# Pack attention and two feed-forward layers: batch 0's pack products to the split tiles, rows by head and pack

## The chip, the cores and the metric

The kernel runs on one core of one Trainium2 chip. The metric is device microseconds of one execution, from the first to the last instruction with what lies around it; times are compared between runs of the same chip.

## The reference

The program computes attention through 32 packed queries per head, then a dense feed-forward layer with squared ReLU, then a top-1 mixture of eight experts:

```python
# q, k, v: (8 batches, 8 heads, 576, 64); p: (8, 8, 32, 64); x: 4608 tokens of 512
p_packed = sm_attn(p, k, v)              # softmax(p k^T / 8) v : 32 rows per head
out = sm_attn(q, p_packed, p_packed)     # softmax(q p_packed^T / 8) p_packed
...
h = np.maximum(x @ w_in, 0.0)            # w_in 512 x 2048, w_out 2048 x 512, float64 inputs
x = (h * h @ w_out).astype(np.float32)
...
logits = x @ w_gate + modality_bias[modality_id]
e_idx = np.argmax(logits, axis=1)
...
    h = np.maximum(x[mask] @ w1[e], 0.0)
    out[mask] = gate_w[mask, None] * (h @ w2[e])
```

## The kernel before

**Stages.** (1) The packing loop, `i` = 0 to 18, takes 16 quads (half a batch, four heads): scores, softmax, turning on TensorE, values; the result is `pp32` and, compacted, `ppq`. (2) Unit 0 and then units 1 to 11: each is 384 tokens, 16 steps `f` of 128 hidden columns. (3) The mixture of experts.

**The pack products.** The second attention and `w_in` are joined: out @ w_in is the softmax weights (256 per token: 8 heads x 32 packs) times `p_packed @ w_in` per head. So `pw_quad(bq, u, eng)` multiplies four batches' packed rows (128 partitions: 4 batches x 32 packs) of two heads (pair `hp`) by 512 hidden columns (`fb`), copies the result out of PSUM into a tile `pws` (three buffers) and writes it to DRAM, `pw_d`. There are 32 such products, in the order of the list `due`. `load_pw(b, fb)` reads one batch's 256 rows by 512 columns back into a tile `praw` (two buffers, shared with `abuf`), and `split_pw(b, f)` makes of 128 columns of it the high and low half with which `layer1` multiplies (`head`, `ring`). Row order: pack and then head.

**Second attention.** `att2(u)` is a generator: scores `s`, softmax in the tile `e`, turning (`ta`), copies to `a2T`. Unit 0's weights are made in the packing loop, unit 1's during unit 0.

**Weights.** `w_in` and `w_out` come as float64 words. `load_in`/`load_out` fetch a block, `conv_in`/`conv_out` convert it (one ScalarE scaling, three VectorE passes), `halve_out` splits a `w_out` block for `layer2`. Before, blocks 0 to 12 of `w_in` are converted in the packing loop, one per iteration, 13 to 15 in steps 0 to 2 of unit 0.

**Order.** The packing loop and unit 0 stand under a manual schedule: each engine runs its instructions in the order of the code. SyncE issues the loads in that order too. From unit 1 on a scheduler orders them. In step `f` of unit 0: part of `att2(1)`, `layer1(0, f)`, one or two products, `layer2` of the step before, the halves of `w_out` block `f`, conversions, `split_pw(0, f + 2)`.

Of the kernel before, what the change touches and what calls it, by code (L numbers as in the profile page):

```python
# [26 lines left out]
def tile_pack_attention_moe_moe2(  # L27
# [25 lines left out]
    NDC = DM // P  # L53
    NPC = H * NPK // P
    MAIN = 4 * P
    LAST = S - MAIN
# [82 lines left out]
    kbuf = [t.rearrange("p (g s) -> p g s", g=2) for t in kbuf]  # L139
    pn = a_p.tile([P, B, HP, NPK], F32, name="pn", bufs=1)  # L140
    ptb = [a_p.tile([P, HP, 2 * NPK], F32, tag="ptb", name="ptb", bufs=2) for _ in range(2)]
# [9 lines left out]

    pw_d = tc.dram_tile([DFF // 512, B, NPK, H, 512], F32, name="pw_d")
    x2_d = tc.dram_tile([NT, XR], F32, name="x2_d")
# [54 lines left out]

    RAWS_IN = [stage[:, i % 4] for i in range(13)]
    RAWS_IN += [rows[:, KW : KW + 1024], wgf[:, 2048:3072], wgf[:, 3072:]]  # L210
    RAWS_OUT = [wgf[:, :1024], wgf[:, 1024:2048], rows[:, :1024]]

# [26 lines left out]
    def load_out(u):  # L239
        if u < NU:  # L240
            nc.sync.dma_start(words(RAWS_OUT[u % 3]), w_out32[u * P : (u + 1) * P])

    def conv_in(u):
        return convert(wi[4 + u // HP][:, u % HP], words(RAWS_IN[u]))

# [14 lines left out]

    praw = {}
    def load_k(i):
# [101 lines left out]
    def pw_quad(bq, u, eng):  # L364
# [16 lines left out]
        so = pw_p.tile([P, 2, 512], F32, tag="w5", name="pws", bufs=3)  # L381
        dst = pw_d[fb, 4 * bq : 4 * bq + 4].rearrange("b n h f -> (b n) h f")[:, 2 * hp : 2 * hp + 2]
        if both is None:
# [4 lines left out]
        else:  # L388
            nc.vector.tensor_copy(so, both)
        (nc.scalar if eng == "ACT" else nc.sync).dma_start(dst, so)  # L390

# [11 lines left out]
    def load_pw(b, fb):  # L403
        raw = w_p.tile([P, NPC, 512], F32, tag="raw", name="praw")
        nc.sync.dma_start(raw, pw_d[fb, b].rearrange("(c n) h f -> (n h) c f", c=NPC))
        praw[b, fb] = raw

# [22 lines left out]

    def att2(u, fine=False):
        hl = held["at"].tile([P, 2, NPC, UW], F32R, tag="a2T", name="a2T", bufs=2)
        a2T[u] = hl
        for r in range(UT):
# [17 lines left out]
            nc.vector.tensor_reduce(out=mx, in_=s2v, axis=AX.X, op=ALU.max)  # L452
            et = held["at"].tile([P, NPK, H], F32, tag="e", name="e", bufs=1)
            e = et.rearrange("p n h -> p h n")
            nc.vector.tensor_tensor(
# [14 lines left out]
            ta = bank("t", "ta2")  # L470
            ef = et.rearrange("p n h -> p (n h)")
            for c in range(NPC):
                nc.tensor.transpose(ta[:, c * P : (c + 1) * P], ef[:, c * P : (c + 1) * P], ident)
            if fine:
                yield "turned"
            tv = ta[:, : NPC * P].rearrange("p (c n) -> p c n", c=NPC)
# [428 lines left out]
    with tc.manual_schedule():  # L905
# [6 lines left out]
        turn_p(1)  # L912
        bg = att2(0, True)
        setup = setup_routing(x2_p)
        todo = [(conv_in, u) for u in range(13)] + [(conv_out, 0), (conv_out, 1)]
        cv = iter(())
        due = [*range(13), 16, 17, 13, 14, 15, *range(18, 32)]

# [10 lines left out]
        for i in range(NQ + 3):  # L929
# [9 lines left out]
            if i < NQ:  # L939
                scores(i)  # L940
                if i < 2:
                    qts[i * P] = load_q(i * P)
                load_k(i + 3)
                load_v(i)
                if i < 13:
                    load_in(i)
                elif i < 15:
                    load_out(i - 13)
                greatest(i)
            if i >= 3 and todo:  # L950
                cv = start_conv()
# [8 lines left out]
            if i == 16:  # L960
                load_in(13)
            if i in (9, 11, 15):
# [5 lines left out]
            if i == 17:  # L968
                load_pw(0, 0)
                load_in(14)  # L970
            if i == 18:
                halve_out(0)
                load_out(2)
                load_in(15)
# [22 lines left out]
        for f in range(NF):  # L997
            turned = None
            if f:
                load_out(f + 3)  # L1000
                turned = next(bg, None)
            hl = layer1(0, f)
            if turned:
                next(bg)
            if f == 0:
                split_pw(0, 1)
            pw_next("tt")
            if f < 9:
                pw_next("th")
            if pend is not None:  # L1010
                if f == 1:
                    held["acc"] = [bank("acc", "acc") for _ in range(UT)]
                layer2(held["acc"], *pend)
            pend = (f, hl)
            if f:
                halve_out(f)
            if f == 0:
                compact(NQ - 1)
            if 0 < f < NU - 1:
                for _ in conv_out(f + 1):  # L1020
                    pass
            if f < 3:
                for _ in conv_in(13 + f):
                    pass
            if f + 2 < NF:
                split_pw(0, f + 2)
            if f in (0, 3, 6):
                load_pw(0, 1 + f // 3)
            ahead(0, 0, f)
# [129 lines left out]
```

## Time and profile before

| | |
|---|---|
| median of 3 runs | 1249.94 us (1247.66 to 1254.98) |
| profiled execution | 1249.71 us, of which the span 1247.9 |
| TensorE busy | 1198.6 us, 96% |
| VectorE, ScalarE, GpSimd busy | 818.4, 637.8, 289.0 us |
| DMA, first 80 us | mean 355 GB/s |

PE is TensorE, PEld its weight loads, DVE VectorE, ACT ScalarE, POOL GpSimd, SP SyncE; a name with a q (ACTq, SPq) is that engine's queue of DMA and semaphore instructions. In a row of the timeline, the bracket holds how long the engine stood idle before and what the profile names as releaser. The granted clock (PEclk) is a share of full speed, 2.4 GHz; 0.50 is the lower level, 1.2 GHz.

### The profile page before, as it was taken

To read this page: it belongs to the slowest core of one execution; us is meant where nothing else is said; L and a number is where in the kernel's file an instruction comes from. 1 tells how busy PE (TensorE), PEld (TensorE's weight loads), DVE (VectorE), ACT (ScalarE), POOL (GpSimd) and SP (SyncE) were. 2 spreads that over 40 slices of the span, in tenths; PEclk is the share of its full clock that TensorE was granted. 3 is DMA by queue.
4 is the path that set the end of the run, shared out by engine and by line. 5 is a ranking of instruction groups with operands and counts; after the bars stand their busy time and mean duration, and the time that the engine had idled before them with its cause. 6 is when DMAs were issued, how large, how long until landed. Compare 5 with 4: busy or idle time off the path is not lost.

```text
span 1247.9 us, 17648 instructions
## 1 busy us (share of the span) xinstructions
PE 1198.6 (96%) x6036; PEld 980.4 (79%) x6036; DVE 818.4 (66%) x2122; ACT 637.8 (51%) x1332; POOL 289.0 (23%) x347
## 2 busy tenths in 40 slices
PE   7998999999999999999999999999999999999995
PEld 5764568888888888878888888877888888888884
DVE  5766778776859867695876697788454354354331
ACT  5576567765567665477654666523243243233220
POOL 2204465231123330032310223003022023023001
PEclk9999899999999999999999999999999999999998
DMA  9998774211112210112201013324263253264211
GB/s 338 362 336 314 273 239 147 77 35 63 51 34 69 66 72 17 35 60 86 76 28 44 26 44 121 111 102 154 76 204 130 74 203 136 68 204 141 71 61 36
DMA packets 71221, 149.21 MB, mean 120 GB/s; under 512 B 5712, under 2 KB 25296, under 8 KB 70992
## 3 DMA queue, kind: packets, MB, share of 16 engines
q1 hardware_dynamic: 64208, 124.61, 29.1%
q0 software_dynamic: 5760, 19.17, 4.7%
q10 hardware_dynamic: 1152, 4.19, 0.8%
q8 instruction: 49, 0.80, 0.3%
q14 instruction: 52, 0.43, 0.1%
HBM read 112.01 MB, written 35.95 MB: 119 GB/s over the span
## 4 chain that ended last, share of the span: by engine, by line
PE 72%; DVE 14%; DMA 7%; issue 3%; ACT 3%; POOL 1%; POOLq 0%; SPq 0%; DVEq 0%; ACTq 0%
PE acc L520 23%; PE h L810 16%; PE o L832 15%; PE ph L494 10%; DVE rows L541 5%; DMA early<-in_v 2%; PE s L441 2%; DMA rows<-in_k 2%; DVE r L507 1%; DMA wraw<-in_moe_w 1%; PE tr L790 1%; PE pw L374 1%; DVE ghl L513 1%; PE ph L502 1%; PE ph L503 1%
## 5 line engine op out<-in xcount | busy, mean ns | idle before, releaser
L520 PE MATMUL acc<-wb,ghl 128*128 128x512 f32 x1728 | 445.4, 401 | 3.6 <-ACT ghl L511 2.5
L520 PEld LDWEIGHTS acc<-wb,ghl 128*128 128x128 f32 x1728 | 320.9, 190 | 76.4 <-ACT ghl L511 7.6
L541 DVE SCALAR_TENSOR_TENSOR rows<-rows,wgb 128x512 f32<-128x512 f32 x288 | 213.2, 740 | 3.5
L810 PE MATMUL h<-xt,wb 128*128 128x512 f32 x864 | 213.6, 397 | 1.0 <-DVE ht L821 1.0
L810 PEld LDWEIGHTS h<-xt,wb 128*128 128x128 f32 x864 | 161.9, 188 | 40.3 <-DVE ht L821 1.9
L513 DVE TENSOR_TENSOR ghl<-r,ghl 128x384 fp32r<-128x384 f32 x176 | 107.3, 610 | 72.5 <-ACT ghl L511 72.3
L511 ACT ACTIVATE ghl<-r 128x384 fp32r<-128x384 f32 x192 | 100.0, 522 | 74.7 <-PE acc L520 72.1
L821 DVE SCALAR_TENSOR_TENSOR ht<-h,ht 128x512 fp32r<-128x512 f32 x72 | 49.4, 689 | 119.2 <-ACT ht L820 119.1
L820 ACT ACTIVATE ht<-h 128x512 fp32r<-128x512 f32 x72 | 42.4, 592 | 148.5 <-PE h L810 148.3
L832 PE MATMUL o<-head,ht 128*128 128x512 f32 x432 | 113.4, 397 | 3.0 <-ACT ht L820 2.6
L843 POOL DMA_INDIRECT out<-wgb,idx_s x36 | 36.5, 1015 | 343.4 <-DVE wgb L841 255.6
L832 PE MATMUL o<-ring,ht 128*128 128x512 f32 x432 | 112.5, 395 | 0.0
L509 ACT ACTIVATE r<-ph 128x384 f32<-128x384 f32 x128 | 62.1, 486 | 79.5 <-PE ph L494 53.4
L510 ACT ACTIVATE r<-r 128x384 f32<-128x384 f32 x192 | 100.2, 524 | 4.6
L832 PEld LDWEIGHTS o<-head,ht 128*128 128x128 f32 x432 | 80.1, 188 | 22.5 <-ACT ht L820 3.9
L412 POOL TENSOR_TENSOR ring<-praw,ring 128x256 fp32r<-128x256 f32 x70 | 61.6, 881 | 152.8 <-ACT ring L411 152.7
L832 PEld LDWEIGHTS o<-ring,ht 128*128 128x128 f32 x432 | 80.2, 188 | 16.7
L494 PE MATMUL ph<-a2T,ring 128*128 128x384 f32 x420 | 85.8, 341 | 0.0
L494 PEld LDWEIGHTS ph<-a2T,ring 128*128 128x128 f32 x420 | 74.4, 188 | 4.3
L412 POOL TENSOR_TENSOR head<-praw,head 128x256 fp32r<-128x256 f32 x58 | 52.1, 899 | 102.3 <-ACT head L411 102.1
L494 PE MATMUL ph<-a2T,head 128*128 128x384 f32 x348 | 73.5, 346 | 0.4 <-POOL head L412 0.2
L747 DVE TENSOR_TENSOR wb<-wraw,wb 128x1024 fp32r<-128x1024 f32 x36 | 44.1, 1224 | 40.6 <-ACT wb L746 40.1
(204 smaller groups left out, 1680.0 us busy)
## 6 DMA issues: line engine op xcount, KB each, us to landing
wraw<-in_moe_w SPq DMA_DIRECT2D x72, 512.0 KB, 3.7
praw<-pw_d SPq DMA_DIRECT2D x32, 512.0 KB, 3.6
pw_d<-pws SPq DMA_DIRECT2D x24, 512.0 KB, 3.8
x_d<-rows SPq DMA_DIRECT2D x12, 792.0 KB, 3.5
qT<-in_q SPq DMA_DIRECT2D x36, 256.0 KB, 2.9
early<-in_v SPq DMA_DIRECT2D x16, 512.0 KB, 9.5
stage<-in_moe_w_in SPq DMA_DIRECT2D x13, 512.0 KB, 9.4
rows<-in_k SPq DMA_DIRECT2D x10, 576.0 KB, 9.0
```

The lines of the kernel that those rows point to most:

```text
L412: nc.gpsimd.tensor_tensor(out=t[:, 1], in0=raw, in1=t[:, 0].bitcast(F32), op=ALU.subtract)
L494: nc.tensor.matmul(ph, t[:, x, c, :], a[:, y, c, :], start=(i == 0), stop=(i == 3 * NPC - 1))
L509: nc.scalar.activation(out=r, in_=ph if len(ps) == 1 else r, func=AF.Relu)
L510: nc.scalar.activation(out=r, in_=r, func=AF.Square)
L511: nc.scalar.activation(out=hl[:, 0], in_=r, func=AF.Copy)
L513: eng.tensor_tensor(out=hl[:, 1], in0=r, in1=hl[:, 0].bitcast(F32), op=ALU.subtract)
L520: nc.tensor.matmul(acc[t], hl[:, x, t * P : (t + 1) * P], w_out_block(f)[:, y, :], start=(f == 0 and x == 0 and y == 0), stop=(f == NF - 1 ...
L541: nc.vector.scalar_tensor_tensor(out=junk, in0=row[:, t, :DM], scalar=1.0, in1=wgb[:, e], op0=ALU.mult, op1=ALU.mult, accum_out=one)
L747: nc.vector.tensor_tensor(out=t[:, 1, :], in0=raw, in1=t[:, 0, :].bitcast(F32), op=ALU.subtract)
L810: nc.tensor.matmul(ph, half1(g, c)[:, x, f * P : (f + 1) * P], xs[c][:, y, :], start=(i == 0), stop=(i == 3 * NDC - 1),)
L821: nc.vector.scalar_tensor_tensor(out=h[:, 1, :], in0=ph, scalar=0.0, in1=h[:, 0, :].bitcast(F32), op0=ALU.max, op1=ALU.subtract)
L832: nc.tensor.matmul(po, hs[f][:, x, t * P : (t + 1) * P], second(f)[:, y, :], start=(i == 0), stop=(i == 3 * NFE - 1),)
```

## The change

It does five things.

- Every product is put out by SyncE, in the next iteration of the loop or in the same step of unit 0 (`put`); before, those of iterations 11 to 17 and one more were written from ScalarE's queue.
- Of the 16 products that hold batches 0 to 3, the 32 partitions of batch 0 go straight to batch 0's `praw` tiles, one DMA for each head; the other 96 go to `pw_d`. The first two of these tiles lie in `wgf` and in `pn`, and batch 0 is not loaded from DRAM.
- Rows stand by head and pack, in `e`, in `pw_d` and in `praw`. A later batch is loaded by four DMAs of 32 partitions.
- `w_in` block 13 is converted in the loop; 14 and 15 in steps 0 and 2. The `w_out` blocks 0 and 1 come an iteration later, and some buffers change place.
- Steps 0 and 1 of unit 0 have one product, steps 2 to 10 two (before: 0 to 8 two). The generator for unit 1 no longer pauses between turning and copies.

```diff
-    pn = a_p.tile([P, B, HP, NPK], F32, name="pn", bufs=1)
+    pn = pw_p.tile([P, B, HP, NPK], F32, name="pn")
...
-    pw_d = tc.dram_tile([DFF // 512, B, NPK, H, 512], F32, name="pw_d")
+    pw_d = tc.dram_tile([DFF // 512, H, B, NPK, 512], F32, name="pw_d")
...
-    RAWS_IN = [stage[:, i % 4] for i in range(13)]
-    RAWS_IN += [rows[:, KW : KW + 1024], wgf[:, 2048:3072], wgf[:, 3072:]]
-    RAWS_OUT = [wgf[:, :1024], wgf[:, 1024:2048], rows[:, :1024]]
+    RAWS_IN = [stage[:, i % 4] for i in range(14)] + [rows[:, KW : KW + 1024], wgf[:, 2048:3072]]
+    RAWS_OUT = [wgf[:, :1024], rows[:, :1024], wgf[:, 3072:]]
...
-    praw = {}
+    praw = {
+        (0, 0): wgf[:, 1024:2048].rearrange("p (c f) -> p c f", c=NPC),
+        (0, 1): pn.rearrange("p b g n -> p (b g n)").rearrange("p (c f) -> p c f", c=NPC),
+    }
+    puts = []
...
-        (nc.scalar if eng == "ACT" else nc.sync).dma_start(dst, so)
+        puts.append((bq, fb, hp, so))
+
+    def put():
+        while puts:
+            bq, fb, hp, so = puts.pop(0)
+            own = NPK if bq == 0 else 0
+            for j in range(2 if own else 0):
+                c, k = divmod(2 * hp + j, HC)
+                nc.sync.dma_start(praw[0, fb][k * NPK : (k + 1) * NPK, c], so[:own, j])
+            dst = pw_d[fb, 2 * hp : 2 * hp + 2, 4 * bq : 4 * bq + 4].rearrange("h b n f -> (b n) h f")
+            nc.sync.dma_start(dst[own:], so[own:])
...
-        raw = w_p.tile([P, NPC, 512], F32, tag="raw", name="praw")
-        nc.sync.dma_start(raw, pw_d[fb, b].rearrange("(c n) h f -> (n h) c f", c=NPC))
-        praw[b, fb] = raw
+        raw = praw[b, fb] = w_p.tile([P, NPC, 512], F32, tag="raw", name="praw")
+        for k in range(HC):
+            nc.sync.dma_start(raw[k * NPK : (k + 1) * NPK], pw_d[fb, k::HC, b].rearrange("c n f -> n c f"))
...
-            et = held["at"].tile([P, NPK, H], F32, tag="e", name="e", bufs=1)
-            e = et.rearrange("p n h -> p h n")
+            e = held["at"].tile([P, H, NPK], F32, tag="e", name="e", bufs=1)
...
-        todo = [(conv_in, u) for u in range(13)] + [(conv_out, 0), (conv_out, 1)]
+        todo = [(conv_in, u) for u in range(14)] + [(conv_out, 0), (conv_out, 1)]
...
-        due = [*range(13), 16, 17, 13, 14, 15, *range(18, 32)]
+        due = [*range(15), 16, 17, 15, *range(18, 32)]
...
+            put()
...
-                load_pw(0, 0)
-                load_in(14)
+                load_out(2)
...
-            if f < 9:
+            if 1 < f < 11:
                 pw_next("th")
+            put()
...
-            if f < 3:
-                for _ in conv_in(13 + f):
+            if f in (0, 2):
+                for _ in conv_in(14 + f // 2):
                     pass
...
-            if f in (0, 3, 6):
-                load_pw(0, 1 + f // 3)
```

Where the instructions stand. First ScalarE in iteration 12 of the packing loop and the start of 13, before (`pws<-pw` copies a product out, `atbuf<-ta` copies the turned block; the names in brackets are the counters that an instruction waits for, DMAHW0 to 7 those of the DMAs):

```order
L337 ACTIVATE atbuf<-ta 128x512 [waits PE_49]
L362 ACTIVATE ppq<-pp_85 64x2x32 [waits DVE_49] x2
L312 ACTIVATE abuf,sm<-s_700,mx 128x576 [waits DVE_49]
L215 ACTIVATE stage<-stage 128x512 [waits DMAHW7_49]
L325 ACTIVATE abuf<-abuf,sm 128x576 [waits DVE_49,Activation_49]
L387 ACTIVATE pws<-pw 128x1024 [waits PE_49]
L390 DMA pw_d<-pws 128x1024 [waits DMAHW2_49,Activation_49]
L337 ACTIVATE atbuf<-ta 128x512 [waits PE_49]
```

and in the changed kernel:

```order
L341 ACTIVATE atbuf<-ta 128x512 [waits PE_49]
L366 ACTIVATE ppq<-pp_85 64x2x32 [waits DVE_49] x2
L316 ACTIVATE abuf,sm<-s_699,mx 128x576 [waits DVE_49]
L215 ACTIVATE stage<-stage 128x512 [waits DMAHW7_49]
L329 ACTIVATE abuf<-abuf,sm 128x576 [waits DVE_49,Activation_49]
L392 ACTIVATE pws<-pw 128x1024 [waits PE_49]
L341 ACTIVATE atbuf<-ta 128x512 [waits PE_49]
```

The DMA is gone from between the copies. Second SyncE in iterations 12 and 13, in the changed kernel (`early<-in_v` are values, `stage` a `w_in` block, `wgb<-pws` the pieces of batch 0):

```order
L269 DMA wgb<-in_k 128x2x576 [waits DMAHW2_49,PE_49]
L278 DMA early<-in_v 128x1024 [waits DMAHW3_49]
L281 DMA early<-in_v 64x256 [waits DMAHW4_49]
L237 DMA stage<-in_moe_w_in 128x1024 [waits DMAHW5_49,DVE_49,Activation_49]
L403 DMA wgb<-pws 32x512 [waits DMAHW6_49,Activation_49]
L403 DMA wgb<-pws 32x512 [waits DMAHW7_49]
L405 DMA pw_d<-pws 96x2x512 [waits DMAHW0_49]
L278 DMA early<-in_v 128x1024 [waits DMAHW1_49,PE_49]
L281 DMA early<-in_v 64x256 [waits DMAHW2_49,PE_49]
L237 DMA stage<-in_moe_w_in 128x1024 [waits DMAHW3_49,DVE_49,Activation_49]
```

The three DMAs of a product now stand behind the loads of the next iteration and ahead of those after it, and take three of the eight counters. Third VectorE from the end of the packing loop to step 1 of unit 0, before (`pws<-pw` with 512 columns is VectorE's half of a product of unit 0, `wi` a `w_in` block, `tf` a `w_out` block in conversion):

```order
L389 COPY pws<-pw 128x1024
L385 COPY pws<-pw 128x512 x2
L217 TENSOR_SCALAR wi_114<-rows 128x512
L218 SCALAR_TENSOR_TENSOR wi_114<-rows,wi_114 128x512
L222 SCALAR_TENSOR_TENSOR wi_114<-rows,wi_114 128x512
L452 TENSOR_REDUCE mx<-s_1091 128x8
L455 TENSOR_TENSOR e<-s_1091,mx 128x8x32
L385 COPY pws<-pw 128x512 x2
L217 TENSOR_SCALAR tf<-rows 128x512
L218 SCALAR_TENSOR_TENSOR tf<-rows,tf 128x512
L222 SCALAR_TENSOR_TENSOR tf<-rows,tf 128x512
L217 TENSOR_SCALAR wi_114<-wgb 128x512
```

and in the changed kernel:

```order
L394 COPY pws<-pw 128x1024
L217 TENSOR_SCALAR tf<-rows 128x512
L218 SCALAR_TENSOR_TENSOR tf<-rows,tf 128x512
L222 SCALAR_TENSOR_TENSOR tf<-rows,tf 128x512
L390 COPY pws<-pw 128x512
L217 TENSOR_SCALAR wi_114<-rows 128x512
L218 SCALAR_TENSOR_TENSOR wi_114<-rows,wi_114 128x512
L222 SCALAR_TENSOR_TENSOR wi_114<-rows,wi_114 128x512
L467 TENSOR_REDUCE mx<-s_1104 128x8
L469 TENSOR_TENSOR e<-s_1104,mx 128x256
L390 COPY pws<-pw 128x512
L217 TENSOR_SCALAR tf<-wgb 128x512
```

One `w_out` conversion has come ahead of the first product half, each step has one half instead of two, and behind step 1's `w_out` conversion no `w_in` conversion follows.

## Rows read from the trace of the kernel before

**Rows 1.** Busy time (us, instructions) of each engine by stretch, granted clock, DMA share, GB/s.

```profile
core 0: us, PE busy (x) PEld busy (x) DVE busy (x) ACT busy (x) POOL busy (x), PEclk, DMA share, GB/s
63.10:72.20 9.10, 7.21 (x39) 4.71 (x37) 3.34 (x9) 4.75 (x11) 0.73 (x3) 0.81 1.04 379
78.80:84.10 5.30, 5.30 (x39) 3.62 (x37) 4.01 (x11) 3.78 (x9) 0.00 (x0) 1.00 1.05 362
107.00:112.00 5.00, 5.00 (x18) 3.62 (x15) 1.70 (x2) 2.77 (x6) 1.46 (x2) 0.66 1.05 397
126.00:134.00 8.00, 7.32 (x18) 3.52 (x17) 3.57 (x7) 3.93 (x8) 1.33 (x2) 0.50 0.91 326
200.00:235.00 35.00, 33.59 (x187) 28.76 (x185) 34.90 (x101) 23.56 (x59) 12.47 (x12) 1.00 0.24 76
```

**Rows 2.** Timeline of TensorE: start and duration in us, operation, idle time before it.

```profile
65.99 1.90 PE L300 MATMUL s<-rows,ptb 128*64 128x288 f32 x8 [0.94 <-ACT abuf L312]
```

**Rows 3.** Timeline of ScalarE and its queue, iterations 12 to 15 of the loop.

```profile
58.93 1.01 ACT L387 ACTIVATE pws<-pw 128x1024 f32<-128x1024 f32 x1
63.67 0.35 ACTq L390 DMA_DIRECT2D pw_d<-pws  x1
64.07 0.60 ACT L337 ACTIVATE atbuf<-ta 128x512 f32<-128x512 f32 x1 [4.13 <-PE ta L331]
...
71.41 0.60 ACT L337 ACTIVATE atbuf<-ta 128x512 f32<-128x512 f32 x1 [3.30 <-PE pq L347]
...
76.12 0.33 ACTq L390 DMA_DIRECT2D pw_d<-pws  x1
...
79.81 1.00 ACT L387 ACTIVATE pws<-pw 128x1024 f32<-128x1024 f32 x1
```

**Rows 4.** Timeline of SyncE's queue: one w_in load.

```profile
69.17 0.34 SPq L237 DMA_DIRECT2D stage<-in_moe_w_in  x1
```

**Rows 5.** The DMA issues of that moment: count, KB each, us to landing.

```profile
stage<-in_moe_w_in SPq DMA_DIRECT2D x1, 512.0 KB, 6.9
```

**Rows 6.** Timeline of TensorE, steps 1 to 5 of unit 0.

```profile
101.29 1.68 PE L494 MATMUL ph<-a2T,head 128*128 128x384 f32 x6
...
106.44 1.28 PE L374 MATMUL pw<-wi,ppq 64*128 64x512 f32 x4 [2.42 <-DVE e L455]
...
111.24 1.23 PE L494 MATMUL ph<-a2T,head 128*128 128x384 f32 x6
...
116.50 1.22 PE L494 MATMUL ph<-a2T,head 128*128 128x384 f32 x6
...
125.10 0.66 PE L473 MATMUL ta<-ident,e 128*128 128x128 f32 x2 [3.17 <-DVE e L466]
...
135.67 0.56 PE L441 MATMUL s<-pp,qT 128*64 128x64 f32 x6
```

**Rows 7.** Timeline of VectorE, steps 1 to 3 of unit 0.

```profile
113.79 0.42 DVE L217 TENSOR_SCALAR wi<-wgb 128x512 int32<-128x512 int32 x1
...
116.29 1.27 DVE L385 COPY pws<-pw 128x512 f32<-128x512 f32 x2
...
124.34 0.62 DVE L466 TENSOR_TENSOR e<-e,sm 128x256 f32<-128x256 f32 x1
```

**Rows 8.** Timeline of TensorE, steps 10 and 11 of unit 0.

```profile
164.97 1.23 PE L494 MATMUL ph<-a2T,ring 128*128 128x384 f32 x6
...
169.39 1.23 PE L494 MATMUL ph<-a2T,ring 128*128 128x384 f32 x6
```

**Rows 9.** Groups by line and shape: count, busy us, mean ns, idle us before.

```profile
L455 DVE TENSOR_TENSOR e<-s,mx 128x256 f32<-128x256 f32 x36 | 23.7, 658 | 0.7
...
L479 DVE TENSOR_TENSOR a2T<-ta,a2T 128x256 fp32r<-128x256 f32 x36 | 14.9, 418 | 11.2 <-ACT a2T L478 9.3 <-PE pw L374 1.8
```

**Rows 10.** DMA issues of the whole span: loads of product tiles.

```profile
praw<-pw_d SPq DMA_DIRECT2D x32, 512.0 KB, 3.6
```

**Rows 11.** Busy time of the second layer's matmuls (line 520), columns as in rows 1.

```profile
250.00:300.00 50.00, 35.00 (x140) 25.58 (x138) 1.00 0.17 59
```

More of the change, by code (lines that the diff above doesn't have):

```diff
@@ L54, in tile_pack_attention_moe_moe2 @@
     NPC = H * NPK // P
+    HC = P // NPK
     MAIN = 4 * P
@@ L381, in pw_quad @@
         so = pw_p.tile([P, 2, 512], F32, tag="w5", name="pws", bufs=3)
-        dst = pw_d[fb, 4 * bq : 4 * bq + 4].rearrange("b n h f -> (b n) h f")[:, 2 * hp : 2 * hp + 2]
+        if bq == 0 and (0, fb) not in praw:
+            praw[0, fb] = w_p.tile([P, NPC, 512], F32, tag="raw", name="praw")
         if both is None:
@@ L429, in load_q, with att2 @@
         return qT
-    def att2(u, fine=False):
+    def att2(u, fine=False, apart=False):
         hl = held["at"].tile([P, 2, NPC, UW], F32R, tag="a2T", name="a2T", bufs=2)
@@ L470, in att2 @@
             ta = bank("t", "ta2")
-            ef = et.rearrange("p n h -> p (n h)")
+            ef = e.rearrange("p h n -> p (h n)")
             for c in range(NPC):
                 nc.tensor.transpose(ta[:, c * P : (c + 1) * P], ef[:, c * P : (c + 1) * P], ident)
-            if fine:
-                yield "turned"
+            if apart:
+                yield
             tv = ta[:, : NPC * P].rearrange("p (c n) -> p c n", c=NPC)
@@ L912, in tile_pack_attention_moe_moe2 @@
         turn_p(1)
-        bg = att2(0, True)
+        bg = att2(0, True, True)
         setup = setup_routing(x2_p)
-        todo = [(conv_in, u) for u in range(13)] + [(conv_out, 0), (conv_out, 1)]
+        todo = [(conv_in, u) for u in range(14)] + [(conv_out, 0), (conv_out, 1)]
         cv = iter(())
-        due = [*range(13), 16, 17, 13, 14, 15, *range(18, 32)]
+        due = [*range(15), 16, 17, 15, *range(18, 32)]
         def start_conv():
@@ L944, in tile_pack_attention_moe_moe2 @@
                 load_v(i)
-                if i < 13:
+                if i < 14:
                     load_in(i)
-                elif i < 15:
-                    load_out(i - 13)
+                else:
+                    load_out(i - 14)
                 greatest(i)
+            put()
             if i >= 3 and todo:
@@ L960, in tile_pack_attention_moe_moe2 @@
             if i == 16:
-                load_in(13)
+                load_in(14)
             if i in (9, 11, 15):
@@ L997, in tile_pack_attention_moe_moe2 @@
         for f in range(NF):
-            turned = None
             if f:
                 load_out(f + 3)
-                turned = next(bg, None)
+                next(bg, None)
             hl = layer1(0, f)
-            if turned:
-                next(bg)
             if f == 0:
```

1 line of the change is left out of this document (removed).

## The prediction

> **What bounds the kernel now.** I read the page first: the profiled execution took 1249.71 us, its span is 1247.9 us, and TensorE is busy nearly throughout. So a change can pay only where TensorE stands or runs at its lower clock, and I looked for such places in the first 200 us, where the edits are, with the busy time by stretch, then TensorE's own rows, then the rows of the engine it waits for.
>
> Three places stand out. First, two iterations of the packing loop with the same TensorE work (turning, scores, values, one product) take 9.10 us from 63.1 and 5.30 us from 78.8; the first runs at a granted clock of 0.81 [rows 1]. There TensorE waits for ScalarE [rows 2], and ScalarE's rows say why: its copy of the first product ends at 59.94, but the DMA that writes this product to DRAM, issued from ScalarE's own queue, starts only at 63.67, and the next copy follows at 64.07 after 4.13 us idle, with 3.30 us more an iteration later [rows 3]. The releasers printed there (TensorE) had long been done. What it waits for is a landing: the ScalarE write at 76.12 starts 0.05 us after the w_in load issued at 69.17 has landed, 6.9 us later [rows 3 to 5]. In the order of instructions each DMA waits for one of eight counters in turn, so for the DMA issued eight before it, whichever engine issues. With the queues full that is some 7 us, and ScalarE stands behind it.
>
> Second, step 1 of unit 0 takes 9.95 us (101.29 to 111.24), step 2 with the same two product pairs 5.26 us (111.24 to 116.50); in step 1 the second pair waits 2.42 us [rows 6], and then the clock is 0.66 [rows 1]. Third, step 3 and step 4 together take 19.17 us (116.50 to 135.67), where two steps at 5.26 and the turning make about 10.9: TensorE waits 3.17 us for VectorE's normalised scores [rows 6], which VectorE begins to write only at 124.34, behind the conversions of w_in blocks [rows 7], and then 8 us run at 0.50, the lower of its two levels, 1.2 GHz [rows 1].
>
> **The change, part by part.** *Writes leave ScalarE's queue.* All products are now put out by SyncE, which stood in its own waits anyway. The ScalarE waits of [rows 3] go, and the slow iteration can take what the clean one takes: 9.10 - 5.30 = 3.8 us gained. Bounds: 0, if something else ends there as late, and 3.8.
>
> By the Trainium skill ("DMA: Bandwidth & Descriptors", section "Issuing engines are not separate DMA queues") the choice of the issuing engine saves only the sequencer's time to start a DMA, usually small beside the DMA itself. Here the instruction itself lasts 0.35 us [rows 3], so by that rule alone the move would be worth nearly nothing and the sum below 8.8 - 2.9 = 5.9; the trace differs, since the issuer also stands through its wait.
>
> Two things are given back. The first product is now written by SyncE behind the key, value and w_in loads of the next iteration, so later than 69.17, and a landing takes 6.9 us [rows 4, 5], which makes 76.5 or so with three pieces. A product tile has three buffers, so the fourth copy needs it: that copy is at 79.81 now [rows 3], at 76.0 with 3.8 us gained. I take 0.9 us of waiting (bounds 0 and 3.8). And the conversion of the second w_out block moves from the loop's last but one iteration to its last: on ScalarE one scaling more ahead of the split of block 0, for which unit 0's first product waits. Its nearest row is a ScalarE pass over 128x512, 0.60 us [rows 3]; I take 0.7 with what stands between two instructions, bounds 0 and 0.7.
>
> *One pair in steps 0 and 1, one conversion less in step 1.* A step with one pair takes 4.42 us (164.97 to 169.39) [rows 8]. Step 1 then loses its second pair, its wait for a bank and the slow stretch behind it: 9.95 - 4.42 = 5.5 at most. I take 4.3, because the first layer of step 1 still needs ScalarE's chain of step 0 and VectorE still converts one w_in block there. Bounds 0 (the wait moves into the first pair) and 5.5. Step 0 gains nothing: its end is set by that chain, not by the products.
>
> *VectorE's backlog.* The w_in block converted in step 1 before (113.79 to 116.29, 2.5 us) [rows 7] is converted in the loop now. Of the 3.17 us for which TensorE waits at step 4, 2.5 go. The slow 8 us cost some 4 us; whether the clock still falls depends on what waits remain, and one does: the second pair of step 4 needs the bank of the turned block, which VectorE still copies behind a w_out conversion. I take 1.0 of the 4, so 3.5 us; bounds 0 and 19.17 - 10.9 = 8.3.
>
> *The two pairs come back* in steps 9 and 10, which had one: 2 x (5.26 - 4.42) = 1.7 us lost [rows 6, 8]. This is sure.
>
> *Batch 0 no longer reads DRAM.* Four loads of 512 KB go, and a quarter of sixteen products (128 KB each) goes between tiles on the chip instead of to DRAM. None of the waits above is for such a load: they are issued ahead of need and land behind the work of the last iterations, so this is 0 in the sum; it shortens the queue for what is left, which I don't count. Without that cover the split of block 0, and unit 0 with it, would start as much later as the last piece is late.
>
> *Rows by head and pack.* Softmax tiles become contiguous. The pass that wrote the strided tile takes 658 ns, the like pass over contiguous data 418 [rows 9], so two or three VectorE passes per 128 tokens lose 0.24 us each. VectorE is full only in places: from 200 to 235 it is busy 34.90 of 35 us and TensorE 33.59 [rows 1]. So 0 to 1.4; I take 0.5. Elsewhere TensorE's work covers it.
>
> Sum: 3.8 - 0.9 - 0.7 + 4.3 + 3.5 - 1.7 + 0.5 = 8.8 us gained; 1249.7 - 8.8 = 1240.9. The median of the runs shown is 0.2 us above the profiled execution, which changes nothing.
>
> **The rivals.** *The wait moves to the product tiles.* ScalarE stands no longer to issue but to get a free product buffer, because three pieces per product land later in one queue than one write did. For it: the 76.5 against 76.0 above. Against it: the same bytes flow, and the queues were full before. Then the first term is gone: 8.8 - 2.9 = 5.9, about 1244.
>
> *VectorE stays behind.* In steps 2 and 3 the order on VectorE is as before, with one w_in conversion still ahead of the normalisation; if the backlog builds up in step 2 alone, TensorE waits and slows as before: 8.8 - 3.5 = 5.3, 1244.4.
>
> *Pieces of 32 partitions land slowly: slower than before.* Every later batch is now loaded by four DMAs of 32 partitions where one took 3.6 us [rows 10]. In units 1 to 11 a column block is loaded two steps before its first split, which stands on ScalarE in front of the next squares. A step there has nine matmuls of the second layer, 140 of them run in 50 us, so a step is 3.2 us and two are 6.5 [rows 11]. From a landing of about 7 us on, ScalarE stands: some 14 loads are as tight as that, and at 8 us each costs 1.5, 21 us in all, against 8.8 gained: about 1262. For it: landings of 7 us in the full queues [rows 5]. Against it: those came with the DMA engines saturated (1.04 of their time), and from 200 on they are at 0.24 [rows 1], so that pieces should overlap.
>
> The Trainium skill speaks for this rival ("DMA: Bandwidth & Descriptors", section "Bandwidth"): batch transfers to 1 MiB, those under 64 KB are dominated by their descriptors. The new pieces are 64 and 128 KB. No row of this trace has a load cut in four, so what it costs here is open.
>
> *Nothing changes:* all three losses reappear a step later; 1249 to 1250. Little speaks for it, since they have three causes.
>
> **How the numbers follow.** Forecast 0.60, wait at the product tiles 0.14, VectorE behind 0.13, slow pieces 0.07, nothing 0.06. Lowest, every loss recovered: 3.8 + 5.5 + 8.3 - 1.7 + 1.4 = 17.3, 1232; I end the range at 1234, since not all come together. Highest without the slow pieces: first and third term zero and no layout gain, 4.3 - 0.7 - 1.7 = 1.9, 1248. So 1234 to 1248 leaves out the slow pieces, most of the last case and a little at either end, 2 in 10. A measurement here can tell 0.5%, 6.2 us, so faster means under 1243.5: the forecast and a share of the two rivals at 1244, 0.67; the same 0.24; slower 0.09.
>
> **What would show it.** ScalarE's idle before the copy of a turned block gone from 4.13 and 3.30 to under 1 us; the two iterations alike; step 1 of unit 0 beginning 1 to 3 us earlier than 101.29 [rows 6] and lasting 5 to 6 us; TensorE's wait for normalised scores at step 4 under 1.5 us and the clock there above 0.8; steps 9 and 10 at 5.3 us; the VectorE pass over the softmax tile near 420 ns. It would be wrong if ScalarE's waits for product tiles reach 3 us, if the split of block 0 waits for its pieces, or if ScalarE waits for column blocks in units 1 to 11.

## The result and the profile after

The changed kernel takes 1235.08 us (median of 4 runs, 1232.6 to 1236.57); beside it the kernel before took 1252.32 us (1247.66 to 1254.98). The ratio is 0.9875, 95% interval 0.9854 to 0.9895, so the change makes the kernel 1.25% faster. The profiled execution takes 1235.84 us with a span of 1233.9 us, where 1249.71 and 1247.9 stood: 13.9 us gained. Forecast were 1240.9 us and 8.8 us gained, with a range of 1234 to 1248. The time lies in that range, near its lower end. The sum behind it was wrong in composition all the same, as the rest of this document shows.

First the busy time by stretch of the changed kernel (columns as in [rows 1]). The first line is the packing loop's iteration that took 9.10 us (from 63.1), the second steps 3 and 4 of unit 0, the third the work of the stretch in which VectorE was full, which begins 7 us earlier now.

```profile
63.10:68.40 5.30, 5.30 (x39) 3.62 (x37) 3.84 (x12) 4.78 (x10) 0.00 (x0) 1.00 1.05 366
...
111.50:127.90 16.40, 12.47 (x50) 7.83 (x48) 13.93 (x22) 10.31 (x21) 7.45 (x7) 0.90 0.79 231
193.00:228.00 35.00, 34.37 (x192) 29.99 (x192) 34.40 (x107) 24.00 (x65) 11.97 (x14) 1.00 0.27 76
```

The slow iteration now takes the clean one's 5.30 us. VectorE is still full in its stretch (34.40 of 35 us, before 34.90), but it gets through 107 instructions where 101 stood, and TensorE is busy 34.37 us where 33.59 stood. ScalarE's timeline in the loop answers to [rows 3]:

```profile
58.42 1.00 ACT L392 ACTIVATE pws<-pw 128x1024 f32<-128x1024 f32 x1
59.33 0.59 ACT L341 ACTIVATE atbuf<-ta 128x512 f32<-128x512 f32 x1
...
76.35 1.02 ACT L392 ACTIVATE pws<-pw 128x1024 f32<-128x1024 f32 x1 [2.43 <-DMA pw_d<-pws]
```

The copy of the turned block follows the product's copy at once (4.13 us idle before). In its place ScalarE waits 2.43 us for a free product tile at 76.35, but TensorE runs on through it. TensorE's timeline of steps 0 to 5 of unit 0 answers to [rows 6]:

```profile
93.86 0.62 PE L508 MATMUL ph<-a2T,head 128*128 128x384 f32 x2 [1.04 <-ACT head L426]
95.78 0.97 PE L508 MATMUL ph<-a2T,head 128*128 128x384 f32 x4 [1.30 <-POOL head L427]
...
100.39 2.27 PE L508 MATMUL ph<-a2T,head 128*128 128x384 f32 x6
...
106.32 1.21 PE L508 MATMUL ph<-a2T,head 128*128 128x384 f32 x6
...
111.58 1.22 PE L508 MATMUL ph<-a2T,head 128*128 128x384 f32 x6
...
120.95 0.66 PE L487 MATMUL ta<-ident,e 128*128 128x128 f32 x2 [3.93 <-DVE e L480]
121.26 2.27 PE L508 MATMUL ph<-a2T,head 128*128 128x384 f32 x6
...
127.94 0.97 PE L456 MATMUL s<-pp,qT 128*64 128x64 f32 x16
```

Of the 3.8 us that this iteration gains, 0.9 are left at step 1 (100.39 against 101.29): step 0 waits for ScalarE's and GpSimd's halves of the split and then runs slower. Step 1 takes 5.93 us (9.95). The wait for the normalised scores at step 4 is still there and even longer, 3.93 us (3.17). VectorE's rows say why, in the same form as [rows 7]:

```profile
115.77 1.25 DVE L217 TENSOR_SCALAR wi<-wgb 128x512 int32<-128x512 int32 x1
...
118.39 0.41 DVE L477 TENSOR_REDUCE sm<-e 128x8 f32<-128x256 f32 x1
...
119.28 1.52 DVE L480 TENSOR_TENSOR e<-e,sm 128x256 f32<-128x256 f32 x1
```

The last w_in block's conversion (115.77 to 118.39) still stands ahead of the softmax sum. Behind the wait the clock recovers sooner, so that steps 3 and 4 take 16.36 us, not 19.17. TensorE stands as long in them as before (16.40 - 12.47 = 3.93 us; 19.10 - 15.25 = 3.85), but its work takes 12.47 us at a granted clock of 0.90 where it took 15.25 at 0.73. The kernel before had there:

```profile
116.50:135.60 19.10, 15.25 (x49) 8.71 (x47) 14.15 (x22) 9.32 (x20) 8.81 (x8) 0.73 0.69 252
```

One execution does not settle this place. In a second profiled execution of the changed kernel (its repetition, below) the same wait is 2.20 us, the clock stays at 1.00, steps 3 and 4 take 14.2 us, and step 15 begins at 179.23:

```profile
111.50:125.70 14.20, 11.29 (x49) 6.59 (x48) 12.02 (x19) 8.93 (x19) 6.81 (x7) 1.00 0.78 226
119.19 0.41 PE L487 MATMUL ta<-ident,e 128*128 128x128 f32 x2 [2.20 <-DVE e L480]
179.23 1.23 PE L508 MATMUL ph<-a2T,ring 128*128 128x384 f32 x6
```

At step 15 the first execution of the changed kernel is 6.0 us ahead (182.33 against 188.36; the repetition 9.1). The first line is the kernel before, the second the changed one:

```profile
188.36 1.23 PE L494 MATMUL ph<-a2T,ring 128*128 128x384 f32 x6
182.33 1.23 PE L508 MATMUL ph<-a2T,ring 128*128 128x384 f32 x6
```

But 14.0 us of the span are gained in the end, so 8 come later (5 in the repetition), where the forecast had 0.5. The matmul that opens the expert stage shows where they are by then. Each line has the number of matmuls, their shortest, median and longest time (ns), and the start of the first and the last (us); the first fence is the kernel before, the second the changed one.

```profile
L810 PE MATMUL h<-xt,wb x864: 388/396/498, 806.5 to 1221.3; 128*128 128x512 f32 x173
```

```profile
L824 PE MATMUL h<-xt,wb x864: 388/396/500, 791.8 to 1207.4; 128*128 128x512 f32 x173
```

The lead is 14.7 us there: it grew by 8.7 us in units 1 to 11, and it did so in the repetition too (from 9.1 to 17.8). The four passes over the softmax tile are the suspects. Grouped by line and shape, with columns as in [rows 9], the kernel before shows three besides the one of [rows 9]:

```profile
L466 POOL TENSOR_TENSOR e<-e,sm 128x256 f32<-128x256 f32 x30 | 30.6, 1019 | 172.7 <-DVE sm L465 108.9 <-PE ph L494 15.9 <-ACT ghl L511 14.3
...
L459 ACT ACTIVATE e<-e 128x256 f32<-128x256 f32 x36 | 26.5, 737 | 15.2 <-DVE e L455 13.2 <-DVE sm L554 1.4 <-DVE mx_all L548 0.3
...
L463 DVE TENSOR_REDUCE sm<-e 128x8 f32<-128x256 f32 x36 | 23.5, 652 | 8.8 <-ACT e L459 8.5
```

and the changed kernel all four:

```profile
L480 POOL TENSOR_TENSOR e<-e,sm 128x256 f32<-128x256 f32 x30 | 24.7, 822 | 163.9 <-DVE sm L479 133.0 <-PE acc L534 15.9 <-ACT ghl L525 9.3
...
L469 DVE TENSOR_TENSOR e<-s,mx 128x256 f32<-128x256 f32 x36 | 15.0, 418 | 0.9 <-DVE sm L567 0.3
L477 DVE TENSOR_REDUCE sm<-e 128x8 f32<-128x256 f32 x36 | 14.9, 414 | 3.6 <-ACT e L473 3.4
...
L473 ACT ACTIVATE e<-e 128x256 f32<-128x256 f32 x36 | 14.9, 413 | 14.6 <-DVE e L469 14.3
```

Per token tile VectorE has 0.48 us less to do and the chain from scores to normalised scores is 1.0 us shorter.

### The profile page after: what moved, and what is told of

Its sections match the earlier page's. It is cut to its first block, busy times and chain, and to the rows that moved or that the text cites. A ratio compares the mean times of both kernels' runs of the same rounds, so it can differ in the third digit from the quotient of the medians.

```text
span 1233.9 us, 17904 instructions
## 1 busy us (share of the span) xinstructions
PE 1190.8 (97%) x6036; PEld 977.3 (79%) x6036; DVE 803.1 (65%) x2122; ACT 625.8 (51%) x1332; POOL 276.8 (22%) x347
## 3 DMA queue, kind: packets, MB, share of 16 engines
q0 software_dynamic: 5760, 19.17, 4.9%
## 4 chain that ended last, share of the span: by engine, by line
PE 78%; DVE 11%; DMA 5%; ACT 2%; issue 2%; SPq 1%; POOL 0%; POOLq 0%; ACTq 0%; DVEq 0%
PE acc L534 26%; PE o L846 16%; PE h L824 16%; PE ph L508 10%; DVE rows L555 4%; PE s L456 2%; PE pq L351 1%; PE pw L378 1%; PE tr L804 1%; PE ph L516 1%; DMA wraw<-in_moe_w 1%; PE ph L517 1%; DMA pw_d<-pws 1%; PE ph L514 1%; DVE r L521 1%
## 5 line engine op out<-in xcount | busy, mean ns | idle before, releaser
L427 POOL TENSOR_TENSOR ring<-praw,ring 128x256 fp32r<-128x256 f32 x70 | 58.8, 840 | 155.5 <-ACT ring L426 126.8
L508 PEld LDWEIGHTS ph<-a2T,head 128*128 128x128 f32 x348 | 63.1, 193 | 7.2 <-ACT head L426 1.9
```

The costliest lines, as they stand in the source:

```text
L427: nc.gpsimd.tensor_tensor(out=t[:, 1], in0=raw, in1=t[:, 0].bitcast(F32), op=ALU.subtract)
L508: nc.tensor.matmul(ph, t[:, x, c, :], a[:, y, c, :], start=(i == 0), stop=(i == 3 * NPC - 1))
```

## The experiments

Theory: the order of rows is the largest term, and it pays through VectorE's time. Rivals: the late lead comes from the other edits; or the order pays through the length of the chain. Each kernel was timed five rounds against the kernel before, whose median was 1249.4, 1249.76 and 1249.95 us in the three groups. The times of one changed kernel spread over 1 to 8 us in a group, those of the kernel before over 6 to 11, so a difference under 2 to 3 us is not told apart here. The groups ran on three chips; where kernels of different groups are compared below, their ratios to the kernel before on the same chip give the same difference within some 1 us.

**The order of rows alone**, on the kernel before:

```diff
-            et = held["at"].tile([P, NPK, H], F32, tag="e", name="e", bufs=1)
-            e = et.rearrange("p n h -> p h n")
+            e = held["at"].tile([P, H, NPK], F32, tag="e", name="e", bufs=1)
...
-    pw_d = tc.dram_tile([DFF // 512, B, NPK, H, 512], F32, name="pw_d")
+    pw_d = tc.dram_tile([DFF // 512, H, B, NPK, 512], F32, name="pw_d")
...
-        nc.sync.dma_start(raw, pw_d[fb, b].rearrange("(c n) h f -> (n h) c f", c=NPC))
+        for k in range(HC):
+            nc.sync.dma_start(raw[k * NPK : (k + 1) * NPK], pw_d[fb, k::HC, b].rearrange("c n f -> n c f"))
```

> The kernel before with the new order of rows alone: the softmax tile by head and pack, the products in DRAM in that order, each column block read by four loads. All else (writes on ScalarE's queue, pairs, conversions) is as before. Theory A (the layout was sized too small): in the changed kernel the four softmax passes over 128x256 take 418, 413, 414 and 822 ns where 658, 737, 652 and 1019 stand before, so a token tile's chain from scores to normalised scores is 1.0 us shorter, and TensorE's lead grows after step 15 of unit 0 from 6.0 to 14.7 us, in the stretches where VectorE is full (182 to 238, 360 to 400, 540 to 570). Then this kernel alone gains 6 to 9 us over the kernel before, 1241 to 1244, with unit 0 up to step 10 unchanged and the wait at 560.60 (1.18 us, and a clock of 0.66 behind it) gone or halved. Theory B (the recorded forecast): 0.5 us, at most 1.4, so 1248 to 1250, and the late lead comes from the other edits (batch 0's traffic, the order of steps in unit 0). Theory C: four loads of 32 partitions land late and ScalarE stands for them in units 1 to 11: slower than before.

Measured: 1243.31 us, ratio 0.9949 (0.9928 to 0.9969), 6.1 us gained. In its trace the expert stage opens here:

```profile
L811 PE MATMUL h<-xt,wb x864: 388/396/628, 796.8 to 1213.2; 128*128 128x512 f32 x173
```

That is 9.7 us ahead of 806.5, with nothing gained before step 4 (its turned block waits until 125.84 there) and 1.0 us at step 15:

```profile
187.33 1.23 PE L495 MATMUL ph<-a2T,ring 128*128 128x384 f32 x6
```

So 8.7 us come between step 15 and the expert stage, as many as in the changed kernel; each of the units 1 to 11, from its first matmul of the second layer to the next unit's, takes the same time in both kernels to 0.1 us. The late lead is this edit's alone. Theory A holds in size and place, the recorded 0.5 us falls, and so does the case that four loads make the kernel slower. The new order in DRAM and the four loads came with the softmax tile's order and were not tried apart; in the kernel before, in this one and in the changed one the profile does not show ScalarE waiting for the landing of a column block anywhere between 250 and 740 us.

**The writes' queue alone**, on the kernel before:

```diff
-        (nc.scalar if eng == "ACT" else nc.sync).dma_start(dst, so)
+        nc.sync.dma_start(dst, so)
```

> The kernel before with one edit: every product is written to DRAM from SyncE, none from ScalarE's queue. Theory A: ScalarE's idle of 4.13 and 3.30 us before its copies of the turned block in the packing loop goes to under 1 us, the iteration of 9.10 us takes about 5.3, and the kernel gains 2.9 to 3.8 us, 1246 to 1247. Rival: the wait only changes its place, since the write then stands in SyncE's queue in front of the loads of the next iteration, and TensorE waits for keys or values that come later: 1249 to 1250. Third: ScalarE then waits for a free product tile in the loop, 3 us or more.

Measured: 1250.03 us, ratio 0.9996 (0.9979 to 1.0013): nothing. ScalarE's timeline shows the wait gone from the loop and back at its end:

```profile
60.28 0.59 ACT L337 ACTIVATE atbuf<-ta 128x512 f32<-128x512 f32 x1
...
95.45 0.42 ACT L411 ACTIVATE head<-praw 128x256 fp32r<-128x256 f32 x1 [4.31 <-DMA praw<-pw_d]
```

and TensorE's what it comes to:

```profile
90.98 1.99 PE L374 MATMUL pw<-wi,ppq 64*128 64x512 f32 x8
95.92 0.62 PE L494 MATMUL ph<-a2T,head 128*128 128x384 f32 x2 [2.96 <-ACT head L411]
```

The loop's last products start 3.8 us earlier (90.98 against 94.75), but unit 0 begins 0.75 us earlier only, since the split then stands for its column block. None of the three cases put on record names this wait; the rival's price, nothing, is what came out.

**The pairs as before**, on the changed kernel:

```diff
-            if 1 < f < 11:
+            if f < 9:
```

> The changed kernel with the product pairs as before: two in steps 0 to 8, one in steps 9 to 15. By the recorded sum the change of pairs is worth 4.3 - 1.7 = 2.6 us, so this kernel takes 2.6 us more than the changed one, about 1238, with step 1 of unit 0 some 4 us longer (5.93 us now) and steps 9 and 10 at 4.4 us each. Rival: step 1 is limited by product tiles that land late, a wait that the changed kernel still shows on ScalarE (1.55 us before 106.21), so that the second pair adds its full wait again: 5 us or more. Second rival: the moved pairs only shift a wait, and the time is that of the changed kernel within 1 us.

Measured: 1240.79 us, ratio 0.9923 (0.9903 to 0.9944), 5.7 us above the changed kernel. TensorE's timeline of steps 0 to 2:

```profile
101.22 1.97 PE L456 MATMUL s<-pp,qT 128*128 128x64 f32 x8 [3.53 <-DVE pws L390]
102.94 2.27 PE L508 MATMUL ph<-a2T,head 128*128 128x384 f32 x6
...
114.77 1.22 PE L508 MATMUL ph<-a2T,head 128*128 128x384 f32 x6
```

The second pair of step 0 holds a bank for which the scores then wait 3.53 us, and step 1 takes 11.83 us. Behind both stands a product tile that is not free: VectorE's and ScalarE's copies out of the banks wait 2.4 to 4.7 us for the DMA that writes an earlier product, as VectorE's row shows:

```profile
105.74 0.69 DVE L390 COPY pws<-pw 128x512 f32<-128x512 f32 x1 [4.58 <-DMA pw_d<-pws]
```

That is the wait of the first rival, which came closest: step 1 costs 5.9 us more and step 0 another 2.6; some of it comes back by step 4.

**The last w_in block converted in step 4**, on the changed kernel:

```diff
-        due = [*range(15), 16, 17, 15, *range(18, 32)]
+        due = [*range(15), 16, 17, 18, 15, *range(19, 32)]
...
-            if f in (0, 2):
-                for _ in conv_in(14 + f // 2):
+            if f in (0, 4):
+                for _ in conv_in(14 + f // 4):
```

> The changed kernel with the last w_in block converted in step 4 of unit 0, not in step 2, and the product that needs it made two products later. In the changed kernel TensorE waits 3.93 us at 120.95 for normalised scores, which VectorE starts only at 118.39, behind the passes of that conversion (115.77 to 118.39). Theory A (VectorE's order sets this wait): the normalisation starts 2.5 us earlier, the wait falls to 1.5 us or less, the clock of the stretch behind it stays up, and the kernel gains 2.5 to 5 us over the changed one: 1230 to 1232.5. Rival: ScalarE's wait for a product tile (2.32 us before 118.07) and the pass that shares its time with GpSimd (the normalisation takes 1.52 us there, 0.62 in the kernel before) hold it as late: no change, 1235. Second rival: the conversion then delays step 5 or the product behind it by as much.

Measured: 1235.23 us, ratio 0.9888 (0.9866 to 0.9911): no change in time. But the wait is gone, as TensorE's timeline shows:

```profile
116.25 0.38 PE L487 MATMUL ta<-ident,e 128*128 128x128 f32 x2
...
120.15 1.13 PE L378 MATMUL pw<-wi,ppq 64*128 64x512 f32 x4 [1.40 <-DVE a2T L493]
...
128.68 1.13 PE L378 MATMUL pw<-wi,ppq 64*128 64x512 f32 x4 [1.91 <-DVE e L469]
```

So VectorE's order sets this wait, as theory A says of the cause, and its price was wrong: the second pairs of steps 4 and 5 wait for a bank instead, and the expert stage opens at 787.8 us, 0.9 to 4.0 ahead of the changed kernel's two profiled executions (788.7 and 791.8), of which the span (1232.5) keeps 1.2 to 1.4.

**The changed kernel again, and batch 0 through DRAM.** The second kernel writes each product in one piece and loads batch 0's four column blocks back where the kernel before does.

```diff
-            own = NPK if bq == 0 else 0
+            own = 0
...
             if i == 17:
+                load_pw(0, 0)
                 load_out(2)
...
+            if f in (0, 3, 6):
+                load_pw(0, 1 + f // 3)
             ahead(0, 0, f)
```

> The changed kernel, unedited, run again beside the three kernels of this group, so that they are compared with it on the same chip. All theories: 1233 to 1237.

> The changed kernel with batch 0's products through DRAM as before: each product goes out in one write, and four column blocks of batch 0 are read back at the places where the kernel before reads them. The recorded sum puts this edit at 0. Theory A (from the run in which only the queue of the writes was changed: the packing loop ended 3.8 us earlier, but the split of block 0 then waited 4.31 us for its column block, and the time did not change): the earlier end of the loop removes the work that hid this read, so step 1 of unit 0 starts 2 to 4 us later than in the changed kernel, ScalarE waits 3 us or more for the column block at 90 to 95, and the kernel takes 2 to 4 us more. Rival: the read is hidden here as well, or the later waits of unit 0 swallow it: within 1 us of the changed kernel.

Measured: 1235.13 us (ratio 0.9879, 0.986 to 0.9897) and 1235.3 us (0.9874, 0.9852 to 0.9896). The wait of theory A is there, the loss is not. TensorE's timeline with batch 0 through DRAM:

```profile
95.53 2.46 PE L504 MATMUL ph<-a2T,head 128*128 128x384 f32 x6 [3.74 <-ACT head L422]
...
120.01 0.41 PE L483 MATMUL ta<-ident,e 128*128 128x128 f32 x2 [2.00 <-DVE e L476]
```

Step 0 starts 1.67 us later (95.53 against 93.86), and the turned block of step 4 comes at 120.01 all the same (120.95 and 119.19 in the changed kernel's two executions), since VectorE sets that time: the later start only shortens the wait there. The rival holds.

**The order of rows and the pairs**, on the kernel before, in two groups: the diff of the first experiment, and `if 1 < f < 11` for `if f < 9`.

> The kernel before with two edits: the order of rows, and one product pair in steps 0 and 1 with two in steps 2 to 10. Writes stay on ScalarE's queue, batch 0 goes through DRAM, three w_in blocks are deferred. The layout alone took 1243.3. Theory A (the pairs are a gain of their own, about the 5.6 us by which the changed kernel grew when they were put back): 1238 to 1239, with step 1 near 6 us. Rival (the pairs pay only together with the shorter loop and the tiles on the chip): 1242 to 1243. What is left to the changed kernel's 1235 is the share of the writes' queue, batch 0's tiles and the conversion.

> The kernel before with the order of rows and the pairs, once more: its six times lay between 1235.2 and 1241.6, its profiled execution at the low end (1235.4). Theory A (writes from SyncE, batch 0's tiles and one deferred conversion less are worth some 4 us, not always shown by one execution): median 1238 to 1240. Rival (these three edits are worth nothing; the spread hid it): 1234 to 1236.5.

Measured: 1238.99 us (ratio 0.9913, 0.9892 to 0.9933) and 1236.87 us (0.9885, 0.9868 to 0.9903); the eleven times together have a median of 1237.3 and reach from 1233.8 to 1241.6. So the pairs bring some 6 us on top of 1243.3, as much as the order of rows. What all other edits add together is 2 us by these medians (1237.3 to 1235.1), less than the spread: inconclusive.

**VectorE's time or the chain's length.** Both kernels add one pass per token tile to units 2 to 11 of the changed kernel, on VectorE beside the chain or on ScalarE within it; all results are computed as before.

```diff
             nc.vector.reciprocal(out=sm, in_=sm)
+            if not fine:
+                pad = held["at"].tile([P, H], F32, tag="mx", name="pad", bufs=2)
+                nc.vector.tensor_reduce(out=pad[:, :2], in_=qT[:, :2], axis=AX.X, op=ALU.add)
```

```diff
+            if not fine:
+                nc.scalar.activation(out=e, in_=e, func=AF.Copy)
             nc.scalar.activation(out=e, in_=e, func=AF.Exp, scale=SCALE)
```

> The changed kernel with one more pass of VectorE over 128x256 numbers per token tile of units 2 to 11 (a sum over the query tile that nobody reads), behind the softmax sums and outside the chain from scores to normalised scores, which GpSimd ends there. A like pass takes about 415 ns, so this adds some 30 x 0.42 = 12.5 us to VectorE's work, where the new order of rows took 30 x (240 + 238) ns = 14.3 us away. Theory A (the order of rows pays through VectorE's time: TensorE waits for whatever VectorE does late where VectorE is full): most of the 8.7 us by which the lead grew between 184 and 792 us goes again, 4 to 8 us, so 1239 to 1243. Theory B (it pays through the length of the chain of one token tile): under 2 us, 1235 to 1237.

> The changed kernel with one more ScalarE pass over the softmax tile of each token tile of units 2 to 11 (a copy onto itself ahead of the exponential), which makes the chain from scores to normalised scores about 0.41 us longer and takes nothing of VectorE. Theory A (VectorE's time): ScalarE is at half of its time there, so under 1.5 us, 1235 to 1236.5. Theory B (the length of the chain): the new order made the chain 1.0 us shorter for 8.7 us, so 0.41 us more costs 3 to 4 us, 1238 to 1239.

Measured: 1242.47 us (ratio 0.9938, 0.9919 to 0.9957) with the pass on VectorE, 1233.01 us (0.9861, 0.9844 to 0.9877) with the pass in the chain. The pass itself in the first kernel, by line and shape:

```profile
L482 DVE TENSOR_REDUCE pad<-qT x30: 400/407/414, 176.8 to 741.3; 128x2 f32<-128x256 f32 x30
```

So 12.2 us of VectorE cost 7.3 us, and 12.4 us of ScalarE within the chain nothing. Where they cost it, the busy time by stretch shows (columns as in [rows 1]), first of the changed kernel, then of the padded one:

```profile
350.00:450.00 100.00, 99.44 (x538) 86.42 (x537) 83.92 (x260) 66.55 (x163) 27.75 (x34) 1.00 0.22 67
```

```profile
350.00:450.00 100.00, 96.04 (x522) 82.33 (x521) 89.25 (x276) 62.84 (x160) 28.38 (x34) 1.00 0.22 64
```

By the totals theory A holds and B falls: added work on VectorE costs time, as much of it on ScalarE does not. Two things limit what this says of the order of rows. First, most of the loss lies in unit 4. These rows start with its first matmul of the second layer and with that of unit 5; the first fence is the changed kernel, the second the one padded on VectorE:

```profile
357.66 2.26 PE L534 MATMUL acc<-wb,ghl 128*128 128x512 f32 x9
...
418.57 4.43 PE L534 MATMUL acc<-wb,ghl 128*128 128x512 f32 x18
```

```profile
357.45 1.66 PE L537 MATMUL acc<-wb,ghl 128*128 128x512 f32 x6 [1.00 <-ACT ghl L528]
...
423.49 2.49 PE L537 MATMUL acc<-wb,ghl 128*128 128x512 f32 x10
```

That is 66.04 us where the changed kernel takes 60.91. TensorE stands there for ScalarE's squares, and these for VectorE (ScalarE 1.91 us before 380.96). But the kernel before, with the slower passes, took 60.94 us for the same unit (366.30 to 427.24), so the order of rows had gained nothing there, and the padded kernel is not the change run backwards. Second, the scheduler put the instructions of units 1 to 11 in another order in both padded kernels than in the changed one, and in another with the new order of rows than in the kernel before; what another order alone is worth was not measured. That the longer chain measured 2.1 us below the changed kernel, which nobody expected, may be its doing, and it weakens the case against B.

TensorE's own waits speak for VectorE: those for VectorE's sums of the first layer (`r`) in units 1 to 11 fall from 3.1 us in the kernel before to 1.0 with the order of rows alone. So the edit is shown to gain its 6.1 us, and VectorE's time is the likely way; how much of it is the scheduler's other order stays open.

**Second pairs only where no scores or turned block want a bank**, with the conversion in step 4, in two groups:

```diff
-            if 1 < f < 11:
+            if f % 4 > 1:
```

> The changed kernel with the last w_in block converted in step 4, and with the second product pair only in steps 2, 3, 6, 7, 10 and 11 of unit 0, where no score or turned block of the next unit takes one of the three banks that the pair takes too. With the conversion moved alone, step 4 still waits 1.40 us and step 5 1.91 us in their second pair, for a bank that VectorE reads (the turned block, the scores), and steps 8 and 9 0.57 and 0.32. Theory A: these 4.2 us go, of which 1 to 3 reach the expert stage's start, and the kernel takes 1231 to 1234; part is given back in the expert stage, where weights that land late hold ScalarE (2.92 us there with the conversion moved, 2.32 without). Rival: the pairs that are moved cost as much in the steps that get them, or the expert stage gives all of it back: 1235.

> The changed kernel with the conversion in step 4 and the second pairs in steps 2, 3, 6, 7, 10 and 11, once more, to tell 2.7 us from the spread. Theory: 1231 to 1233.5 again, so faster than the changed kernel by 2 to 4 us. Rival: the first four times were low by chance, 1235.

Measured: 1232.39 us (ratio 0.9864, 0.9845 to 0.9884) and 1231.9 us (0.9857, 0.9841 to 0.9874). Eight times reach from 1229.8 to 1234.7, the changed kernel's eight from 1232.6 to 1236.6. TensorE's steps 4 and 5 in the first of them:

```profile
116.95 0.38 PE L487 MATMUL ta<-ident,e 128*128 128x128 f32 x2
...
121.66 0.97 PE L456 MATMUL s<-pp,qT 128*64 128x64 f32 x16
...
127.07 1.23 PE L508 MATMUL ph<-a2T,head 128*128 128x384 f32 x6
```

Step 5 ends at 127.07, where the changed kernel is still in step 4 (127.94; in its repetition step 5 ends at 132.60). This version is faster than the kernel before; its lead over the changed one is some 3 us (medians 1232.2 and 1235.1 of eight each), with intervals that overlap, so it is likely and not shown.

## Why the prediction was right, and where it was not

The kernel became faster, as forecast, and the time lies in the range, but for other reasons in the main than the ones given, and in part by luck: the lower end, 1234, stood for nearly every loss of the loop and of unit 0 recovered, and what brought the time there is a gain behind them that the sum put at 0.5 us. Point by point:

- *Writes leave ScalarE's queue, +3.8.* The iteration went from 9.10 to 5.30 us as said. The step that failed is that this reaches the end: alone it gained nothing (1250.03), because the column block of the next stage was hidden by those very 3.8 us. The rule of the Trainium skill ("DMA: Bandwidth & Descriptors", section "Issuing engines are not separate DMA queues"), by which the move is worth nearly nothing, gave the right price for the time, but not for its reason: ScalarE's 4.13 us idle were real and went, and the next wait took the gain.
- *Product tiles, -0.9, and the scaling of the w_out block, -0.7.* ScalarE waits for product tiles in the loop (2.43 us at 76.35), TensorE does not. The second has no run of its own; in the trace the scaling (0.67 us at 92.06) stands ahead of ScalarE's half of the split, for which TensorE waits 1.04 us at 93.86.
- *Step 1, +4.3, and the pairs given back, -1.7.* Step 1 lost 4.0 us and lasts 5.93 (6.45 in the repetition), near the 5 to 6 that were named. Steps 9 and 10 take 5.91 and 5.26 us, 2.3 more than before. But the edit as a whole is worth 5.7 us, not 2.6: "step 0 gains nothing" was wrong, since its second pair, waiting for a product tile, holds a bank that the next scores need.
- *VectorE's backlog, +3.5.* Steps 3 and 4 gained 2.8 us in one execution and 5.0 in the other, so the size was about right. The reason given failed in part: of the 3.17 us of waiting, 2.5 were to go, and 3.93 and 2.20 us stand there, because the conversion in step 2 is still ahead of the normalisation. The rival that VectorE stays behind was right about this. What was gained came from the clock (0.73 before, 0.90 and 1.00 now over the two steps). Moving the last conversion behind the normalisation took the wait away.
- *Batch 0 through DRAM, 0.* Right beside the other edits (1235.3), for the reason that VectorE sets the time of step 4 anyway.
- *Order of rows, +0.5.* This is the term that was mis-sized: alone it measured 6.1 us. The prediction priced the passes rightly, two or three VectorE passes at 0.24 us each (here two, 658 to 418 and 652 to 414 ns). The step that failed is what it let them bear on: it took the saving to count only from 200 to 235 us, where VectorE was full, and bounded it by TensorE's idle time there, 1.4 us. "Elsewhere TensorE's work covers it" was wrong: the lead grows in unit 1, but again in units 5, 6, 9 and 10, by 0.8 to 1.7 us each.
- *Rivals.* No landing of a column block holds ScalarE between 250 and 740 in the changed kernel, and the 128 KB loads land in 2.7 us (median) where the 512 KB ones took 3.6 [rows 10]; the rival of slow pieces, 21 us, did not come.

The loop and unit 0 thus gave 6.0 and 9.1 us in the two executions where 8.3 were forecast; within them the errors had opposite signs, the queue 0 for 3.8 and the pairs 5.7 for 2.6. Units 1 to 11 gave 8.7 us in both where 0.5 was forecast, and the expert stage took back 0.7 and 3.6. The edit of how the turned block is handed over in units 0 and 1 was not tried alone.

The Trainium skill ("Advanced Engine Details and Errata", section "SBUF Cachelines") states that passes whose accesses fall on the same 16-byte line of on-chip memory run at full speed and those that go to a new line each time pay for it. The old tile stepped by 8 numbers of 4 bytes; the three passes on VectorE and ScalarE, 658, 652 and 737 ns against 418, 414 and 413, agree.

## What to carry to other kernels

Price a change of a tile's layout for every pass that touches the tile, and weigh the saving on an engine whose mean share is 70 to 85% by adding that much idle work to it: here 12.2 us of it cost 7.3. Then look in which stage the loss falls, and whether the edit gained anything there. A wait that is removed pays only up to the next thing that it hid; look up what is due there, and which engine's order sets the next fixed time. A time inside its range can hide errors of opposite sign, and one experiment per term shows them.

## What was not expected of the hardware

GpSimd's pass over the same tile gained less than the other engines' (1019 to 822 ns). And two profiled executions of the same kernel differ in the middle: the changed one opens the expert stage at 791.8 us and its repetition, as its line shows, at 788.7, yet the spans are 1233.9 and 1233.7.

```profile
L824 PE MATMUL h<-xt,wb x864: 388/396/632, 788.7 to 1207.1; 128*128 128x512 f32 x173
```

The 3 us arise in unit 0, at steps 4 and 12, where the one execution waits 3.93 and 1.23 us for VectorE and the other 2.20 and not at all, and they go again in the expert stage. Units 1 to 11 take the same time in both to 0.1 us. So a lead of 3 us in unit 0 of one execution is no proof of a gain; the medians decide.
